# A feed-forward kernel: the first blocks of x fetched by DMA transpose instead of TensorE transposes, with chunk 1 and the last store rearranged

## The chip, the cores and the metric

The kernel runs on one core of a Trainium2 chip. The metric is the device time of one execution in microseconds (us). "Before" is the kernel as it was, "after" is the changed one.

A ratio is the mean time of one kernel's fast runs over the mean of the other's fast runs of the same rounds, so it is not quite the ratio of the medians that are also quoted. It comes with a 95% interval.

## The reference

```
def reference(x, w_gate, w_up, w_down):
    return (_gelu(x @ w_gate) * (x @ w_up)) @ w_down     # gelu: tanh form
# x: 32 x 32 x 1024, w_gate and w_up: 1024 x 3584, w_down: 3584 x 1024, all bf16
```

The 1024 tokens form two blocks of 512. The 1024 input columns form eight k blocks of 128. The kernel's matmuls contract over the partitions of their operands, so x is needed with its columns on partitions: transposed.

## The kernel before

The kernel multiplies 2 x 2 blocks by a Strassen-like scheme (sums S1 to S4 of the weights, T1 to T4 of x, seven products in place of eight). The first chunk of w_gate and w_up is computed plainly while the sums are formed. Names used below: `b21` holds the last four k blocks of x for the first 512 tokens; it is read first. `b11` holds the first four k blocks, `b12` and `b22` are the second 512 tokens. `a12a` is weights for products that are computed ahead. `w_tiles[0, ...]` is the first chunk of w_gate and w_up. PSUM banks come from three tags, A (4 banks), B (2) and C (2).

The head fetches the first two k blocks of b21 (`KQ = 2`) as they lie in memory and transposes them on TensorE. The other six come by DMA transpose:

```
    with tc.manual_schedule():
        for eng, p0, p1 in ((nc.sync, 0, HALF), (nc.scalar, HALF, NB_P)):
            eng.dma_start(out=x_nat[:, p0:p1, :],
                in_=xf[p0 * P : p1 * P, KD * P : (KD + KQ) * P].rearrange("(b p) d -> p b d", p=P))
        # [cut]
        for k, eng in enumerate((nc.sync, nc.scalar)):
            load_ahead(0, k, k + 1, eng)              # a12a, k block 0 and 1
        for which, eng in enumerate((nc.sync, nc.scalar)):
            load_w(eng, 0, which, KD, KD + KQ)        # w_gate, w_up for these k blocks
        load_xT(0, KD + KQ, DT)                       # DMA transpose, k blocks 2 and 3 of b21
        load_ahead(0, KQ, KD)
        load_w0(nc.sync, KD + KQ, DT)
        load_ahead(1, 0, KD)
        load_xT(0, 0, KD)                             # b11
        # [cut: w, b12, b22]
        warm_ps = acc("A")
        for _ in range(NWARM):                        # 6 matmuls on constants
            nc.tensor.matmul(warm_ps, lhsT=ones_w, rhs=ones_m, start=True, stop=True)
        # [cut: eight 128x128 TensorE transposes of x_nat, copied to b21; one half-size filler matmul]
```

Then the products start, one k block after the other:

```
        for k in range(KQ):
            for j in range(KB):
                product_ahead(ps[j], 0, j, k, k + 1)  # 4 matmuls per k block
        plain0(KD, KD + KQ)                           # 8 matmuls, token block 0
        for j, copy in enumerate((nc.scalar.copy, nc.vector.tensor_copy) * 2):
            product_ahead(ps[j], 0, j, KQ)            # k blocks 2 and 3: "third k block" below
            copy(ahead[0][:, j, :], ps[j])
```

Chunk 1, where the scheme begins, and the last bank of the output:

```
        # [cut: plain products of chunk 0]
        for j, tag in enumerate("BB"):
            ps = acc(tag)
            product_ahead(ps, 2, j)
            nc.scalar.copy(ahead[2][:, j, :], ps)
        tt(t3, b22, b12, SUB)
        begun = [first_product(FC + fl) for fl in range(FC)]   # P1, then added(...) on DVE frees the bank
        next(chunk1)                                           # S3
        tt(t4, b21, t2, SUB)
        # [cut: all chunks; S1 goes to bank C, S2 to the banks of P1]
        for copy, queue, c0 in ((nc.vector.tensor_copy, nc.sync, 0), (nc.scalar.copy, nc.scalar, NB // 2)):
            o = late.tile([P, NB // 2], bf16, name="o_end", tag="o_end", bufs=2)
            copy(o, banka[m][:, c0 : c0 + NB // 2])
            queue.dma_start(out=of[r0 : r0 + P, c0 : c0 + NB // 2], in_=o)
```

## Time and profile before

| | before |
|---|---|
| median of the first 3 runs | 275.81 us (275.01 to 275.81) |
| span in the profile | 273.6 us |
| PE busy | 269.1 us (98%) |
| first real product | 4.58 us |
| third k block starts | 8.03 us |
| last bank's copy starts | 270.02 us |

The profiled execution took 275.36 us, a little under the median.

The page's first part gives, for each engine, busy time, share of the span and instructions; a later line gives DMA packets by size.

```profile
span 273.6 us, 3349 instructions
...
PE 269.1 (98%) x1199; PEld 187.9 (69%) x1199; DVE 198.1 (72%) x195; ACT 111.4 (41%) x183; POOL 108.1 (40%) x55
...
DMA packets 53393, 33.77 MB, mean 123 GB/s; under 512 B 8704, under 2 KB 53376, under 8 KB 53376
```

The view of waits, of PE alone over the whole span, has one line: only the start of the program is waited for.

```profile
PE psA L224 <- PEq L582: 0.8, 1, 0.8
```

The matmuls wait for nothing else; weight loads (PEld) have waits of their own. What is left to win is the head, short stalls and the tail. The timeline shows the head; its columns are start, duration, engine, line, operation, result and operands, count, and in brackets the idle time before and what ended it. SPq and ACTq are the issues of DMAs on the two queues.

```profile
0.77 2.72 PE L224 MATMUL psA<-const-bfloat16-1.0 128*128 128x512 bf16 x6 [0.77 <-PEq L582]
...
2.21 1.56 SPq L205 DMA_TRANSPOSE b<-in_x_dram  x1
...
3.51 0.90 PE L232 MATMUL tp<-ident,x_nat 128*128 128x128 bf16 x8
...
4.58 0.59 PE L273 MATMUL psC<-b,a12a 128*128 128x512 bf16 x2
...
7.98 1.45 PEld L273 LDWEIGHTS <-a12a 128*128 128x128 bf16 x8 [0.28 <-DMA a12a<-in_w_gate_dram]
8.03 1.03 PE L273 MATMUL psC<-b,a12a 128*128 128x512 bf16 x4
```

The six warm-ups take 0.43 us apiece, the products 0.216 us apiece (two in 0.59 us: they start 0.216 us apart, and the record of one lasts 0.38 us). The page's row of granted clock prints full speed from the first slice on, so the slow clock of the start has to be read from such spacings; the trace's clock records (the array `clock` in the packed trace, which no view prints) give full clock from 4.13 us.

Chunk 1 in the timeline: DVE's t3 at 27.91 us stands ahead of the additions at 30.11 us, and the matmul group that needs the banks they free starts 2.27 us after its forerunner (28.57 to 30.84); later in this trace the same step takes 2.02 us where nothing is waited for (36.18 to 38.20). The waits of the weight loads name the cause (PEld, 16 to 50 us):

```profile
PEld psA L258 <- DVE c L335: 0.5, 1, 0.5
```

The timeline of DVE and PE:

```profile
27.91 2.29 DVE L355 TENSOR_TENSOR t<-b,b 128x2048 fp32r<-128x2048 bf16 x1
28.57 2.21 PE L258 MATMUL psC<-t,s 128*128 128x512 f32 x8
30.11 1.28 DVE L335 TENSOR_TENSOR c<-ahead,psA 128x512 f32<-128x512 f32 x2
30.84 2.11 PE L258 MATMUL psA<-t,s 128*128 128x512 f32 x8
```

The tail in the timeline: ACT's half copy waits for DVE's, so the last store is issued at 270.88 us.

```profile
270.02 0.42 DVE L568 CAST o_end<-psA 128x256 bf16<-128x256 f32 x1 [0.90 <-PE psA L421]
270.47 0.36 SPq L569 DMA_DIRECT2D out_dram<-o_end  x1
270.48 0.37 ACT L568 CAST o_end<-psA 128x256 bf16<-128x256 f32 x1 [3.04 <-DVE o_end L568]
270.88 0.34 ACTq L569 DMA_DIRECT2D out_dram<-o_end  x1
```

### The profile page before, as it was taken

The page shows a single profiled execution, that of the slowest core. Times are in us where ns is not written, and L with a number is a line of the kernel's source. Part 1 is how long each engine was busy: PE and PEld are TensorE (multiplying, and loading weights), DVE is VectorE, ACT ScalarE, POOL GpSimd, SP SyncE. Part 2 cuts the span into 40 slices and gives each one's busy share as a digit, 9 for nine tenths or more (in the row PEclk, how much of TensorE's full clock was granted, in tenths as well). Part 3 has the DMA queues.
Part 4 walks back from the last instruction along what each step waited for, and adds up shares of the span by engine and source line. Part 5 has one row for each costly group of instructions (what it writes and reads, how often), then busy time and mean ns, then how long its engine had stood idle before and what let it go on. Part 6 is the DMA issues. An engine that isn't in the chain of part 4 may idle for free.

```text
span 273.6 us, 3349 instructions
## 1 busy us (share of the span) xinstructions
PE 269.1 (98%) x1199; PEld 187.9 (69%) x1199; DVE 198.1 (72%) x195; ACT 111.4 (41%) x183; POOL 108.1 (40%) x55
## 2 busy tenths in 40 slices
PE   8999999999999999999999999999999999999994
PEld 3444677877878677676868676764447888888883
DVE  0269997987966676666657656459999999999511
ACT  2263565454643646555463636430300023962001
POOL 1000089999897695948577574000000000000000
PEclk9999999999999999999999999999999999999999
DMA  7994330414504505050514280004992445695202
GB/s 173 282 240 127 101 90 25 117 42 114 156 16 137 146 8 157 0 153 1 154 35 120 74 274 0 0 2 163 350 293 79 134 134 189 216 285 194 78 0 78
DMA packets 53393, 33.77 MB, mean 123 GB/s; under 512 B 8704, under 2 KB 53376, under 8 KB 53376
## 3 DMA queue, kind: packets, MB, share of 16 engines
q1 hardware_dynamic: 50384, 31.13, 39.4%
q10 hardware_dynamic: 2992, 2.43, 2.7%
q8 instruction: 9, 0.15, 0.2%
q14 instruction: 8, 0.07, 0.1%
HBM read 29.62 MB, written 2.10 MB: 116 GB/s over the span
## 4 chain that ended last, share of the span: by engine, by line
PE 87%; SPq 5%; DVE 4%; DMA 2%; issue 1%; ACT 0%; DVEq 0%
PE psA L258 34%; PE psA L421 18%; PE psC L258 17%; PE psC L421 7%; PE psB L421 7%; PE psB L258 5%; SPq L205 3%; DMA b<-in_x_dram 2%; DVE lo L254 1%; SPq L134 1%; DVE t L355 1%; DVE t L317 1%; SPq L194 1%; DVE s L163 0%; DVE s L162 0%
## 5 line engine op out<-in xcount | busy, mean ns | idle before, releaser
L258 PE MATMUL psA<-t,s 128*128 128x512 f32 x208 | 54.3, 403 | 0.1
L250 ACT ACTIVATE h<-c 128x512 bf16<-128x512 f32 x52 | 31.8, 630 | 38.9 <-DVE c L335 38.9
L258 PEld LDWEIGHTS psA<-t,s 128*128 128x128 f32 x208 | 39.0, 188 | 9.7 <-DVE c L335 0.5
L162 POOL TENSOR_TENSOR s<-wu 128x1024 fp32r<-128x1024 bf16 x12 | 26.8, 2232 | 23.4 <-DMA wu<-in_w_up_dram 14.0
L335 DVE TENSOR_TENSOR c<-sn,psA 128x512 f32<-128x512 f32 x26 | 17.8, 683 | 16.8 <-PE psA L258 16.5
L258 PEld LDWEIGHTS <-wg 128*128 128x128 bf16 x168 | 15.4, 98 | 20.1 <-issue 3.4
L163 POOL TENSOR_TENSOR s<-s,wg 128x1024 fp32r<-128x1024 f32 x12 | 27.8, 2314 | 0.9
L165 POOL TENSOR_TENSOR s<-wg,wu 128x1024 fp32r<-128x1024 bf16 x12 | 27.1, 2255 | 0.0
L340 ACT COPY sn<-psC 128x512 f32<-128x512 f32 x26 | 15.2, 588 | 27.1 <-PE psC L258 23.0
L340 ACT COPY sn<-psA 128x512 f32<-128x512 f32 x42 | 23.4, 585 | 6.2 <-PE psA L258 6.1
L258 PE MATMUL psC<-t,s 128*128 128x512 f32 x104 | 25.9, 391 | 0.0
L258 PE MATMUL psA<-t,a22r 128*128 128x512 f32 x104 | 25.9, 391 | 0.0
L258 PE MATMUL psC<-b22r,s 128*128 128x512 f32 x104 | 25.7, 389 | 0.0
L258 PE MATMUL psA<-b,wg 128*128 128x512 bf16 x104 | 24.6, 380 | 0.0
L258 PEld LDWEIGHTS psC<-t,s 128*128 128x128 f32 x104 | 19.5, 188 | 4.2
L258 PEld LDWEIGHTS psA<-t,a22r 128*128 128x128 f32 x104 | 19.5, 188 | 4.1
L258 PEld LDWEIGHTS psC<-b22r,s 128*128 128x128 f32 x104 | 19.5, 188 | 4.1
L400 DVE TENSOR_TENSOR lo<-c,h 128x512 bf16<-128x512 f32 x12 | 21.5, 1794 | 0.6
L335 DVE TENSOR_TENSOR c<-sn,psC 128x512 f32<-128x512 f32 x26 | 17.7, 687 | 5.1 <-PE psC L258 5.1
L353 DVE TENSOR_TENSOR hi<-h,psA 128x512 bf16<-128x512 bf16 x14 | 9.6, 688 | 14.2 <-PE psA L258 14.2
L164 POOL TENSOR_TENSOR s<-wg,s 128x1024 fp32r<-128x1024 bf16 x8 | 17.3, 2159 | 0.6
L464 ACT COPY snb<-psC 128x512 f32<-128x512 f32 x4 | 2.2, 590 | 36.5 <-PE psC L421 22.7
(101 smaller groups left out, 411.9 us busy)
## 6 DMA issues: line engine op xcount, KB each, us to landing
wu<-in_w_up_dram SPq DMA_DIRECT2D x13, 512.0 KB, 4.0
wdb<-in_w_down_dram SPq DMA_DIRECT2D x12, 512.0 KB, 4.8
wdb<-in_w_down_dram SPq DMA_DIRECT2D x12, 384.0 KB, 4.1
wg<-in_w_gate_dram SPq DMA_DIRECT2D x8, 512.0 KB, 5.1
v<-in_w_down_dram SPq DMA_DIRECT2D x4, 512.0 KB, 6.4
out_dram<-o_sb ACTq DMA_DIRECT2D x15, 128.0 KB, 1.7
wg<-in_w_gate_dram SPq DMA_DIRECT2D x6, 256.0 KB, 4.5
v<-in_w_down_dram SPq DMA_DIRECT2D x4, 384.0 KB, 7.8
```

What stands on the lines that cost most here:

```text
L162: yield eng.tensor_tensor(s1, a21, a22, ADD)
L163: yield eng.tensor_tensor(s2, s1, a11, SUB)
L164: yield eng.tensor_tensor(s4, a12, s2, SUB)
L165: yield eng.tensor_tensor(s3, a11, a21, SUB)
L205: nc.sync.dma_start_transpose(out=t[:, d0 % KD : (d1 - 1) % KD + 1, :], in_=xf[nb * NB : (nb + 1) * NB, d0 * P : d1 * P])
L250: nc.scalar.activation(h, src, ACT.Gelu_apprx_tanh)
L258: nc.tensor.matmul(ps, lhsT=lhs[:, k, :], rhs=rhs[:, k, :], start=(start and k == 0), stop=(k == KD - 1), skip_group_check=True,)
L335: tt(t, s, ps, ADD)
L340: nc.scalar.copy(t, ps)
L353: tt(g_of(ft)[:, :NB], h0, psa, MUL)
L400: tt(g_of(ft)[:, NB:], added(sn5[fl], psa[fl]), h1[fl], MUL)
L421: nc.tensor.matmul(banks[m], lhsT=lhs(k)[:, m * P : (m + 1) * P], rhs=rhs(k), start=(start and k == 0), stop=(k == HF - 1), skip_group_che ...
```

## The change

The intent: fetch the first two k blocks by DMA transpose too, one tile per DMA, with all transposes on the sync queue and the first weights on the scalar queue; this frees TensorE, DVE and ACT of the transposes and their copies. In chunk 1, P1 comes before the products ahead, and its additions before T3, S3 and T4. The last bank is copied and stored whole.

```
-    NWARM = 6
+    NWARM = 7
@@ head
-        for eng, p0, p1 in ((nc.sync, 0, HALF), (nc.scalar, HALF, NB_P)):
-            eng.dma_start(out=x_nat[:, p0:p1, :], ...)
-        for k, eng in enumerate((nc.sync, nc.scalar)):
-            load_ahead(0, k, k + 1, eng)
-        for which, eng in enumerate((nc.sync, nc.scalar)):
-            load_w(eng, 0, which, KD, KD + KQ)
+        for k in range(KQ):
+            load_xT(0, KD + k, KD + k + 1)
+            load_ahead(0, k, k + 1, nc.scalar)
+        load_w0(nc.scalar, KD, KD + KQ)
         load_xT(0, KD + KQ, DT)
-        # the eight TensorE transposes, their four copies, the filler matmul
@@ chunk 0 and 1   [cut: plain_out of token block 1 moved behind t4; its banks A and B, not A and C]
-        tt(t1, b12, b11, SUB)
         for fl in range(FC):
             ...
+            if fl == 0:
+                tt(t1, b12, b11, SUB)
+        p1 = [acc("A") for _ in range(FC)]
+        for fl in range(FC):
+            prod(p1[fl], quads(1, fl)[0], b11, True)
+        for j, tag in enumerate("CC"):
+            ps = acc(tag)
+            product_ahead(ps, 2, j)
+            nc.scalar.copy(ahead[2][:, j, :], ps)
+        begun = [first_product(FC + fl, p1[fl]) for fl in range(FC)]
         tt(t3, b22, b12, SUB)
-        begun = [first_product(FC + fl) for fl in range(FC)]
@@ tail
-            if m < MT - 1: ...            # and the split of the last bank in two halves
+            o = late.tile([P, NB], bf16, name="o_sb", tag="o_sb", bufs=MT)
+            (nc.vector.tensor_copy if m % 2 == 0 else nc.scalar.copy)(o, banka[m])
+            nc.scalar.dma_start(out=of[r0 : r0 + P, :NB], in_=o)
```

More of the change, by code (lines that the diff above doesn't have):

```diff
@@ L6 @@
 from concourse._compat import with_exitstack
-from concourse.masks import make_identity
 ACT = mybir.ActivationFunctionType
@@ L176 @@
     ones_m = nc.const_aps.tensor(1.0, [P, NB], bf16)
-    ident = xpool.tile([P, P], bf16, name="ident")
-    make_identity(nc, ident)
-    NB_P = NB // P
-    HALF = NB_P // 2
-    x_nat = spool.tile([P, NB_P, KQ * P], bf16, name="x_nat", tag="s1")
-    with tc.manual_schedule():
-        for eng, p0, p1 in ((nc.sync, 0, HALF), (nc.scalar, HALF, NB_P)):
-            eng.dma_start(
-                out=x_nat[:, p0:p1, :],
-                in_=xf[p0 * P : p1 * P, KD * P : (KD + KQ) * P].rearrange("(b p) d -> p b d", p=P),
-            )
+    gate = xpool.tile([P, 1], f32r, name="gate")
+    with tc.manual_schedule():
         alloc_w(0, 0)
@@ L224 @@
             nc.tensor.matmul(warm_ps, lhsT=ones_w, rhs=ones_m, start=True, stop=True)
-        tags = iter("CCBB")
-        for dt in range(KQ):
-            for half in range(2):
-                hw = HALF * P
-                tag = next(tags)
-                tp = ps1.tile([P, hw], bf16, name="tp", tag=tag, bufs=BANKS[tag])
-                for b in range(HALF):
-                    nc.tensor.transpose(
-                        tp[:, b * P : (b + 1) * P], x_nat[:, half * HALF + b, dt * P : (dt + 1) * P], ident
-                    )
-                (nc.vector.tensor_copy, nc.scalar.copy)[half](b21[:, dt, half * hw : (half + 1) * hw], tp)
-        nc.tensor.matmul(warm_ps[:, : NB // 2], lhsT=ones_w, rhs=ones_m[:, : NB // 2], start=True, stop=True)
         def plain(ps, which, fl, nb, d0, d1, first=0, last=DT - 1):
@@ L251, in gelu, with plain_out @@
             return h
-        def plain_out(ft, nb, gate, up):
-            tt(g_of(ft)[:, nb * NB : (nb + 1) * NB], gelu(gate, "h0", 4), up, MUL)
+        def plain_out(ft, nb, h, up):
+            tt(g_of(ft)[:, nb * NB : (nb + 1) * NB], h, up, MUL)
         def prod(ps, lhs, rhs, start):
@@ L311 @@
                 plain(tok0[fl][which], which, fl, 0, 0, KD, KD, KD - 1)
-            plain_out(fl, 0, *tok0[fl])
-        tok1 = [(acc("A"), acc("C")) for _ in range(FC)]
+            plain_out(fl, 0, gelu(tok0[fl][0], "h0", 4), tok0[fl][1])
+            if fl == 0:
+                tt(t1, b12, b11, SUB)
+        tok1 = [(acc("A"), acc("B")) for _ in range(FC)]
         for fl in range(FC):
@@ L324 @@
                 plain(tok1[fl][which], which, fl, 1, KD, DT)
-            plain_out(fl, 1, *tok1[fl])
+            tok1[fl] = gelu(tok1[fl][0], "h0", 4), tok1[fl][1]
         load_w_all(2, 1)
-        for j, tag in enumerate("BB"):
-            ps = acc(tag)
-            product_ahead(ps, 2, j)
-            nc.scalar.copy(ahead[2][:, j, :], ps)
         def added(s, ps):
@@ L341, in snap, with first_product @@
             return t
-        def first_product(ft):
-            psa = acc("A")
-            prod(psa, quads(*divmod(ft, FC))[0], b11, True)
+        def first_product(ft, psa=None):
+            if psa is None:
+                psa = acc("A")
+                prod(psa, quads(*divmod(ft, FC))[0], b11, True)
             if ft < FC + NAHEAD:
@@ L353, in last_product @@
             tt(g_of(ft)[:, :NB], h0, psa, MUL)
+        p1 = [acc("A") for _ in range(FC)]
[6 more added lines that the diff above has]
+        begun = [first_product(FC + fl, p1[fl]) for fl in range(FC)]
         tt(t3, b22, b12, SUB)
-        begun = [first_product(FC + fl) for fl in range(FC)]
         next(chunk1)
         tt(t4, b21, t2, SUB)
-        nc.gpsimd.tensor_copy(ident[:, :1], t4[:, 0, :1])
+        nc.gpsimd.tensor_copy(gate, t4[:, 0, :1])
+        for fl in range(FC):
+            plain_out(fl, 1, *tok1[fl])
         open_fts = []
@@ L559 @@
             r0 = NB + m * P
-            if m < MT - 1:
-                o = late.tile([P, NB], bf16, name="o_sb", tag="o_sb", bufs=MT)
-                (nc.vector.tensor_copy if m % 2 == 0 else nc.scalar.copy)(o, banka[m])
-                nc.scalar.dma_start(out=of[r0 : r0 + P, :NB], in_=o)
-                continue
-            for copy, queue, c0 in ((nc.vector.tensor_copy, nc.sync, 0), (nc.scalar.copy, nc.scalar, NB // 2)):
-                o = late.tile([P, NB // 2], bf16, name="o_end", tag="o_end", bufs=2)
-                copy(o, banka[m][:, c0 : c0 + NB // 2])
-                queue.dma_start(out=of[r0 : r0 + P, c0 : c0 + NB // 2], in_=o)
+            o = late.tile([P, NB], bf16, name="o_sb", tag="o_sb", bufs=MT)
+            (nc.vector.tensor_copy if m % 2 == 0 else nc.scalar.copy)(o, banka[m])
+            nc.scalar.dma_start(out=of[r0 : r0 + P, :NB], in_=o)
 _INS = ['x', 'w_gate', 'w_up', 'w_down']
```

## The prediction

> **What bounds the kernel now.** TensorE. The page gives PE 269.1 us busy of a 273.6 us span, and the waits view knows no PE wait on DMA, DVE or ACT. In the timeline matmuls start every 0.216 us (bf16) or 0.227 us (f32) from 4.58 us to 270.0 us. The change removes none of these real matmuls, so it can only move the head (first product at 4.58 us), small stalls between chunks, and the tail (270.0 to 273.6 us).
>
> **The head.** Before: six warm-up matmuls (0.77 to 3.49 us), x_nat lands 2.7 us after issue, eight transposes and a filler fill 3.51 to 4.52 us, product at 4.58. After that the head is paced by loads rather than by the transposes: the first w_gate block lands at about 6.05 (used at 6.10) and the next a12a block at 7.92, where the weight load waits 0.28 us. The DMA engines are saturated from 3 us to 21 us (share 1.0 or more in the windows view).
>
> After the change the first transpose issues at 0.74. The existing two-tile transpose held the queue 1.56 us and its first packets ran 2.0 us after issue (x_nat's: 1.1). I estimate issue 0.8 us per tile, data from 2.7 us, first tile landing at 4.4 (4.0 to 5.0), second near 5.2, the pair near 6.6. The scalar queue's a12a and w blocks no longer wait behind x, so w lands earlier, near 5. First product about 4.6; the next a12a block is issued near 4.0 (before 3.82) and lands at 8.0 to 8.5. In DMA time, x_nat cost 512 packets of 28 ns; two transposed tiles cost 1024 packets of 18 to 39 ns in this trace, over 16 engines 0.3 to 1.5 us more. [...] these packets (256 B at 18 ns against 512 B at 28) show them slower per byte. So removing the PE transposes gains nothing: PE then waits for DMA instead. Head: +0.1 us (-0.3 to +0.7).
>
> **Chunk 1.** DVE's t3 (2.29 us, 27.9 to 30.2) delays the additions; PE's weight load waits 0.50 us for c, matmul S1 to S2 takes 2.27 instead of 2.02 us, so 0.25 us is lost. With P1 before the a12b products, additions run near 26.5 to 27.8, ahead of t3; this wait should vanish. The new bank reuse (ahead copy of C, 0.59 us, before S1 into the same bank) has near 0.1 us slack. Gain 0.2.
>
> **Tail.** The last bank's split copies run one after the other (0.42, 0.37; last store issued at 270.88). One 0.59 us copy lets it issue at 270.6. Gain 0.1 to 0.2.
>
> **Sum.** +0.1 - 0.2 - 0.15: about -0.3 us. I predict 275.5 us (275.81 before; range 274.6 to 276.5). Faster by over 2%: 0.5%; within 2%: 98.5%; slower: 1%.
>
> **What would show it.** First real product between 4.3 and 5.0; PE waiting on DMA (b21 or a12a) in the first 9 us; P1 and S1 of chunk 1 back to back, no wait on c; Pool's sums starting 1 us earlier without effect; last store issued at 270.6 minus the shift; PE still near 98%.
>
> **What would make it wrong.** The first transposes take over 5.5 us to land: the head loses 1 us or more. The warm-up ends at about 3.8 and PE idles; [...] (full clock began at 4.1 us in this trace), so an idle gap could delay full clock [...]. Or the scalar queue's loads arrive so much earlier that PE starts by 4.2 and never waits: 0.5 us gained.

## The result, and the profile after

| | before | after |
|---|---|---|
| median | 275.81 us (275.01 to 276.0, 6 runs) | 276.4 us (276.0 to 277.24, 6 runs) |
| ratio, 95% interval | | 1.0031 [1.001, 1.0052] |
| span in the profile | 273.6 us | 275.4 us |
| first real product | 4.58 us | 4.71 us |
| third k block starts | 8.03 us | 10.37 us |
| S1 to S2 in chunk 1 | 2.27 us | 1.95 us |
| last bank's copy starts | 270.02 us | 272.05 us |
| from there to the end of the span | 3.6 us | 3.4 us |

The change made the kernel 0.6 us slower by the medians, clear of the interval, though far within 2%. The profiled execution of after was the slowest of its six (277.24 us), which matters below. The lines of the page:

```profile
span 275.4 us, 3319 instructions
...
PE 270.4 (98%) x1191; PEld 187.9 (68%) x1191; DVE 192.5 (70%) x192; ACT 111.2 (40%) x181; POOL 106.5 (39%) x53
...
DMA packets 53793, 33.77 MB, mean 123 GB/s; under 512 B 9744, under 2 KB 53776, under 8 KB 53776
```

There are some 1000 more packets under 512 B: two transposed tiles of 512 rows. The waits of PE have a second line now:

```profile
PE psC L252 <- DMA b<-in_x_dram: 0.8, 1, 0.8
PE psA L215 <- PEq L561: 0.8, 1, 0.8
```

The timeline of the head:

```profile
0.74 3.89 SPq L195 DMA_TRANSPOSE b<-in_x_dram  x3
...
0.78 3.14 PE L215 MATMUL psA<-const-bfloat16-1.0 128*128 128x512 bf16 x7 [0.78 <-PEq L561]
...
4.71 1.01 PE L252 MATMUL psC<-b,a12a 128*128 128x512 bf16 x2 [0.79 <-DMA b<-in_x_dram]
...
5.51 1.06 PE L252 MATMUL psA<-b,a12a 128*128 128x512 bf16 x2
...
6.54 1.01 PE L252 MATMUL psC<-b,a12a 128*128 128x512 bf16 x2
...
10.37 1.03 PE L252 MATMUL psC<-b,a12a 128*128 128x512 bf16 x4
```

Pairs of products now take 1.01 to 1.06 us where they took 0.59: they run at half clock. The clock records give full clock from 9.09 us in place of 4.13. Chunk 1 in the timeline, where the wait has gone:

```profile
31.07 2.12 PE L237 MATMUL psC<-t,s 128*128 128x512 f32 x8
33.02 1.98 PE L237 MATMUL psA<-t,s 128*128 128x512 f32 x8
```

The tail in the timeline: one copy, and the store follows 0.61 us after the copy's start (before: 0.86).

```profile
272.05 0.58 ACT L547 CAST o_sb<-psA 128x512 bf16<-128x512 f32 x1 [2.59 <-PE psA L407]
272.66 0.34 ACTq L548 DMA_DIRECT2D out_dram<-o_sb  x1
```

So in this execution the head lost 2.34 us (8.03 to 10.37), chunk 1 won 0.3 and the tail 0.2. Two theories for the head offer themselves, and they are not exclusive. **A**: TensorE sits idle for 0.79 us between the warm-ups and the first product, and that postpones the full clock. **B**: the second transposed tile lands late, so that TensorE would have to wait even at full clock. A rival, **C**, blames the rearranged chunk 1. Where B's cure was tried, a further rival **D** says that all loads of the head are late and the wait only moves.

### The profile page after: what moved, and what is told of

It reads as the page before. It is cut to its first block, busy times and chain, and to the rows that moved or that the text cites. A ratio compares the mean times of both kernels' runs of the same rounds, so it can differ in the third digit from the quotient of the medians.

```text
span 275.4 us, 3319 instructions
## 1 busy us (share of the span) xinstructions
PE 270.4 (98%) x1191; PEld 187.9 (68%) x1191; DVE 192.5 (70%) x192; ACT 111.2 (40%) x181; POOL 106.5 (39%) x53
## 4 chain that ended last, share of the span: by engine, by line
PE 97%; DMA 1%; ACT 0%; issue 0%
PE psA L237 34%; PE psA L407 18%; PE psC L237 17%; PE psC L407 7%; PE psB L407 7%; PE psB L237 5%; PE psA L219 3%; PE psB L219 3%; PE psC L252 2%; PE psA L252 2%; DMA b<-in_x_dram 1%; ACT o_sb L547 0%
## 5 line engine op out<-in xcount | busy, mean ns | idle before, releaser
L386 DVE TENSOR_TENSOR lo<-c,h 128x512 bf16<-128x512 f32 x12 | 18.1, 1509 | 0.6
```

The costliest lines, as they stand in the source:

```text
L386: tt(g_of(ft)[:, NB:], added(sn5[fl], psa[fl]), h1[fl], MUL)
```

## The experiments

Eleven runs were made, all correct, each with 5 or 6 fast executions beside 11 of before (mean of before: 275.78, 275.71 and 275.64 us in the three calls). Names with a_ are edits of after, with b_ of before.

| kernel | median us | mean us | ratio to before [95%] | full clock from, in the profile | third k block |
|---|---|---|---|---|---|
| before (first profile) | 275.81 | 275.64 | | 4.13 us | 8.03 |
| after | 276.4 | 276.50 | 1.0031 [1.001, 1.0052] | 9.09 | 10.37 |
| a_again | 276.22 | 276.46 | 1.0029 [1.001, 1.0047] | 4.34 | 9.13 |
| a_warm9 | 276.13 | 276.22 | 1.0019 [1.0, 1.0037] | 5.82 | 9.13 |
| a_pair | 275.88 | 276.18 | 1.0018 [0.9995, 1.0042] | 3.97 | 9.01 |
| a_fill9 | 275.77 | 275.78 | 1.0004 [0.999, 1.0018] | 6.11 | 8.86 |
| a_pair_w | 275.76 | 275.72 | 1.0002 [0.9987, 1.0016] | 5.82 | 8.86 |
| b_head | 277.67 | 277.67 | 1.007 [1.005, 1.0089] | 9.04 | 10.51 |
| b_head_warm9 | 276.8 | 276.88 | 1.0044 [1.0032, 1.0056] | 3.57 | 9.35 |
| b_warm4 | 276.46 | 276.54 | 1.0028 [1.0009, 1.0048] | 8.54 | 10.06 |
| b_rest | 275.29 | 275.27 | 0.9983 [0.9966, 0.9999] | 6.13 | 8.86 |
| b_rest_again | 275.23 | 275.35 | 0.9989 [0.9977, 1.0002] | 4.94 | 8.29 |
| b_rest_third | 275.11 | 275.13 | 0.9978 [0.9964, 0.9992] | 3.49 | 7.82 |

### b_head and b_rest: which part of the change costs

b_head is before with the hunk of the diff marked "head" and `NWARM = 7` alone. b_rest is before with all the other hunks (chunk 0 and 1, tail), `NWARM = 6` and the old head:

```
b_head = before + (NWARM, head)
b_rest = before + (chunk 0 and 1, tail)
after  = before + (NWARM, head) + (chunk 0 and 1, tail)
```

> The kernel before with only the head of the change (DMA transposes, seven warm-ups). Theory A: the loss is here, 276.5 to 277.2 (0.5 us slower than after, since it lacks the gains of chunk 1 and the tail). Rival B: the same time. Rival C: as before, 275.6 to 276.0.

> The kernel before with only the rest of the change (chunk 1 order and the undivided last store). Theories A and B: faster than before by 0.4 to 0.6 us (0.32 from chunk 1, 0.23 from the tail, as the two traces show), 275.2 to 275.4. Rival C: slower than before by 0.3 to 0.8.

Measured: the head alone costs 0.7%, 1.9 us by the means. The rest alone wins 0.17%, 0.5 us. Theory C falls. But the two do not add up: 1.9 - 0.5 gives 1.4, and after is only 0.75 to 0.86 us slower by the means. Two reasons offer themselves, and neither is shown. The reordering of chunk 1 may be worth more behind the new head; b_head_warm9 below looks like that, but b_head's own profile does not. Its timeline at chunk 1, PE alone:

```profile
31.04 2.19 PE L237 MATMUL psC<-t,s 128*128 128x512 f32 x8
33.07 1.98 PE L237 MATMUL psA<-t,s 128*128 128x512 f32 x8
```

From S1 to S2 that is 2.03 us, with nothing lost. Or the full clock came late more often in b_head: five of its six executions took 277.47 us or more, while in after five of twelve were slow (see a_again). Only one profile of b_head was kept, so this stays open; so does why b_head came out 0.5 us above the range expected for it. (The 0.23 us that the text above gives the tail is too much: from the last copy to the end of the span the two traces show 3.55 and 3.40 us.)

### b_warm4: the gap alone

```
-    NWARM = 6
+    NWARM = 4
```

> The kernel before with four warm-ups in place of six: nothing changes in the loads, but TensorE idles about 1.0 us (2.5 to 3.5 us) before the transposes. Theory A: the full clock starts later than 4.1 us, at 7 to 9 us, in most executions, and the time rises by 0.5 to 1.8 us over before. Rival B: no change (within 0.3), since the first transpose still starts when x lands.

Nothing but two warm-ups was taken from before, and the loads are the same. The timeline of b_warm4, PE alone:

```profile
0.77 1.87 PE L224 MATMUL psA<-const-bfloat16-1.0 128*128 128x512 bf16 x4 [0.77 <-PEq L582]
3.57 1.14 PE L232 MATMUL tp<-ident,x_nat 128*128 128x128 bf16 x8 [0.93 <-DMA x_nat<-in_x_dram]
...
7.28 1.06 PE L273 MATMUL psA<-b,a12a 128*128 128x512 bf16 x2
```

TensorE idles 0.93 us, the first eight products run at half clock (a pair in 1.06 us), the full clock starts at 8.54 us, and the kernel is 0.76 us slower by the means (the profiled execution, 277.04 us, is one of the slower of the six). So an idle stretch of this length in the head can cost time by the clock alone. Theory A's mechanism is there.

### a_warm9: the gap bridged

```
-    NWARM = 7
+    NWARM = 9
```

> The kernel after with nine warm-up matmuls in place of seven, so that TensorE has no idle stretch between the warm-up and the first product. Theory A (the idle 0.79 us delays the full clock): in the profile the products start at the same time (4.6 to 4.8 us) but run at 0.216 us spacing from there or soon after, and the time falls by 0.8 to 1.8 us against after, to 274.6 to 275.6. Rival B (the head is held by the later loads, the clock is only a passenger): the time stays within 0.3 us of after, 276.1 to 276.7, and TensorE waits for a12a, w or b instead. Rival C (the loss is in the reordered chunk 1): also no change.

The gap is gone and the full clock starts at 5.82 us. But the mean falls by 0.28 us only, from 276.50 to 276.22 (0.31 to 0.42 against each one's own runs of before; the intervals overlap), where theory A expected 0.8 to 1.8. The timeline of a_warm9, PE alone, shows why:

```profile
5.59 0.71 PE L252 MATMUL psA<-b,a12a 128*128 128x512 bf16 x2
6.54 0.59 PE L252 MATMUL psC<-b,a12a 128*128 128x512 bf16 x2 [0.24 <-DMA b<-in_x_dram]
...
9.13 1.03 PE L252 MATMUL psC<-b,a12a 128*128 128x512 bf16 x4
```

The products of the second tile start at 6.54 us, the same time as in after. The clock is faster, and TensorE waits for the tile instead. The prediction for a_warm9 was wrong in size, and theory A alone is not enough. It was also held against an execution of after with a late clock, and not all of them have one, as the next run shows.

### a_again: after once more, with a lucky clock

No edit.

> The kernel after, unchanged, to see how its executions spread and a second profile of it. Theory A (the idle gap delays the full clock): the full clock starts at 7.8 us or later in this profile too, and the times lie at 276 to 277.3. Theory B (the second transposed tile lands late, 1.9 us after the first, so that TensorE would wait for it even at full clock): the second product group starts at 6.5 to 6.9 us whatever the clock does; the two are not exclusive.

Theory A's number for this run failed: TensorE was idle for the same stretch (3.91 to 4.72 us), but the full clock came in the middle of it, at 4.34 us. That makes it the cleanest view of theory B, and the right one to hold against the profile of before (full clock at 4.13). The waits of PE, and the timeline of the head:

```profile
PE psC L252 <- DMA b<-in_x_dram: 1.6, 2, 0.8
```

```profile
4.72 0.59 PE L252 MATMUL psC<-b,a12a 128*128 128x512 bf16 x2 [0.80 <-DMA b<-in_x_dram]
...
5.15 0.59 PE L252 MATMUL psA<-b,a12a 128*128 128x512 bf16 x2
...
6.54 0.59 PE L252 MATMUL psC<-b,a12a 128*128 128x512 bf16 x2 [0.80 <-DMA b<-in_x_dram]
...
9.13 1.03 PE L252 MATMUL psC<-b,a12a 128*128 128x512 bf16 x4
```

The first four products are done in 0.86 us, and then the second tile is still 0.8 us away. From 6.54 us the twelve products at 0.216 us give 9.13 us exactly, so no other load holds the head. At full clock the head thus costs 9.13 - 8.03 = 1.10 us. The rest of the two traces: S2 of chunk 1 starts at 31.77 us against 30.84 (now 0.93 behind), the last bank's copy at 270.80 against 270.02 (0.78 behind), and the span ends at 274.2 against 273.6 (0.6 behind). This is 1.10 lost, 0.32 won around chunk 1 (about half of it before S2, the rest in the group after it) and 0.15 won in the tail (with the spans unrounded, 273.574 and 274.199 us). The two profiled executions took 275.36 and 275.98 us. The medians also differ by 0.6 us, but each of them mixes earlier and later clocks, so that the two agree may be chance; by the means, after is 0.86 us slower in the first call and 0.75 in the second.

The twelve executions of after fall into two groups: seven from 275.77 to 276.22 us and five from 276.68 to 277.44. One profile fell into each: 275.98 us with full clock at 4.34, and 277.24 us with full clock at 9.09. Their third k blocks lie 10.37 - 9.13 = 1.24 us apart, their times 1.26 us. So between these two a late clock costs that much on top. That the other ten split for the same reason is likely, but no profile of them was kept. It would also fit a_warm9: its mean, 276.22, lies near that of the fast group, 276.05 (the slow group: 277.07).

### b_head_warm9: the head with the gap bridged, on before

b_head with `NWARM = 9`.

> The kernel before with the head of the change alone and nine warm-ups. Theory A: 0.8 to 1.5 us faster than b_head (277.67 median), 276.2 to 276.9, with the full clock at 4.2 to 7.6 us. Theory B alone: no faster than b_head by more than 0.4 us.

It is 0.79 us faster than b_head by the means (0.72 when each is held against its own runs of before): just short of what theory A expected, and more than theory B alone allowed. The full clock starts at 3.57 us, earlier than expected, in the middle of the warm-ups; so in this profile it does not come from a bridged gap, and TensorE even sits idle from 4.25 to 4.87 us. The timeline of it, PE alone, at chunk 1:

```profile
29.89 2.20 PE L237 MATMUL psC<-t,s 128*128 128x512 f32 x8
32.42 2.12 PE L237 MATMUL psA<-t,s 128*128 128x512 f32 x8 [0.34 <-DVE c L314]
```

Without the reordering of chunk 1, S1 to S2 takes 2.53 us here, 0.50 more than the 2.03 of b_head, where nothing was waited for; before lost 0.25 (2.27 against 2.02). So the two parts of the change are not independent, but how they act on each other depends on the clock: in b_head TensorE reached S1 1.15 us later (31.04 against 29.89), DVE began the additions 0.28 us sooner (31.41 against 31.69), and there was nothing left for the reordering to mend.

### a_pair: one transpose for both tiles

```
-    NWARM = 7
+    NWARM = 10
+        load_xT(0, KD, KD + KQ)
         for k in range(KQ):
-            load_xT(0, KD + k, KD + k + 1)
             load_ahead(0, k, k + 1, nc.scalar)
```

> The kernel after with the first two tiles fetched by one DMA transpose in place of two, and ten warm-ups to bridge until it lands. Theory B: the pair needs one issue (about 1.3 us) instead of two, lands at 5.0 to 5.5 us, the eight first products follow without a gap, and the products of the third and fourth k block start at 8.5 to 8.9 us (9.13 in a_warm9, 7.98 before); the time falls by 0.3 to 0.7 us against a_warm9, to 275.5 to 275.9. Theory A alone: as a_warm9, 276.1 to 276.3.

The issues say why the second tile was late. In after, the three transposes of the head hold the sync queue 1.25, 1.25 and 1.29 us, for one, one and two tiles. So an issue was hardly cheaper here with half the tiles (1.25 against 1.29). They land 3.9, 4.5 and 4.0 us after their issue, at 4.7, 6.5 and 7.3 us. The lines of the first two, from the DMA view (tile, queue, operation, count, us from issue to landing) and, for the second, its issue in the timeline:

```profile
b<-in_x_dram SPq DMA_TRANSPOSE x1, 3.9
...
2.04 1.25 SPq L195 DMA_TRANSPOSE b<-in_x_dram  x1
...
b<-in_x_dram SPq DMA_TRANSPOSE x1, 4.5
```

Of the 1.83 us between the two landings, 1.30 are the distance of the issues and 0.53 the longer way from issue to landing; the packets of the second tile (3.72 to 5.27 us) ran beside those of w_gate and w_up, those of the first (2.16 to 3.18) before them. In a_pair one issue of 1.34 us brings both tiles in 4.3 us, at 5.0 us. The timeline, PE alone:

```profile
5.08 0.59 PE L252 MATMUL psC<-b,a12a 128*128 128x512 bf16 x2 [0.42 <-DMA b<-in_x_dram]
...
6.80 1.03 PE L219 MATMUL psA<-b,wg 128*128 128x512 bf16 x4
8.13 1.04 PE L219 MATMUL psB<-b,wu 128*128 128x512 bf16 x4 [0.30 <-DMA wu<-in_w_up_dram]
9.01 1.03 PE L252 MATMUL psC<-b,a12a 128*128 128x512 bf16 x4
```

The wait for the second tile is gone, as theory B expected. But w_up, from the scalar queue, now lands at 8.1 us (after: 6.2), 6.0 us after its issue (before: 4.5), and the third k block starts at 9.01 us, only 0.12 us sooner. Here rival D was right: the wait moved. In the packet records of the first 8 us, the 512 B packets of the scalar queue take 51 ns apiece by the mean, where in before they took 28; the median is 27 ns in both, so it is some packets that are held up for long. The median time, 275.88 us, is in theory B's range, but one of the six executions took 277.95 us, and the third k block is later than it expected.

### a_pair_w: the order mended

a_pair with the first w blocks on the sync queue, between the pair and the second pair of tiles:

```
-        load_w0(nc.scalar, KD, KD + KQ)
+        load_w0(nc.sync, KD, KD + KQ)
```

> a_pair with the first two w blocks issued on the same queue as the transposes, between the pair and the second pair, in place of the scalar queue, so that they do not share the DMA engines with the second pair. In a_pair the wait had moved to w_up (8.13 us). Theory B with order: w lands at 5.6 to 6.5, no wait, the third k block starts at 8.5 to 8.7 (9.01 in a_pair), the time is 275.5 to 275.8. Rival D (total DMA time): the third k block starts at 8.9 or later because a12a lands late, 275.9 to 276.2.

PE waits for no load any more. The third k block starts at 8.86 us, between the two ranges; but the full clock came at 5.82 us in this profile, and the first two products took 0.85 us in place of 0.43. The pair had landed at 4.55 us already; the ten warm-ups at half clock kept TensorE until 4.99 us. By the means it is 0.46 us faster than a_pair, but by the medians 0.12 (most of the difference is a_pair's one slow execution; ratio 1.0002 against 1.0018, the intervals overlap), so the times decide nothing. Theory B with order fits better than rival D, since no load was waited for.

### a_fill9: only TensorE reordered

```
-    NWARM = 7
+    NWARM = 9
         for k in range(KQ):
             for j in range(KB):
                 product_ahead(ps[j], 0, j, k, k + 1)
-        plain0(KD, KD + KQ)
+            plain0(KD + k, KD + k + 1)
```

> The kernel after with nine warm-ups, and TensorE alone reordered: between the products of the first and of the second tile it now does the four token products that need only the first tile; all loads stay as they are. Theory B (the late second tile is what holds the head at full clock): the four products take 0.86 us of the wait, the third k block starts at 8.3 to 8.7 us in place of 9.13, and the time falls by 0.4 to 0.8 us against a_warm9 (276.22 mean), to 275.4 to 275.8. Rival D (the DMA engines as a whole are late, and the second tile is only the first of many late loads): the wait moves to the next load (w or a12a), the third k block still starts near 9.0, and the time stays at 276.0 to 276.3.

All loads are as in after and a_warm9. TensorE alone does other work while the second tile is on its way. The timeline, PE alone:

```profile
4.75 1.01 PE L252 MATMUL psC<-b,a12a 128*128 128x512 bf16 x2
...
7.13 0.59 PE L252 MATMUL psC<-b,a12a 128*128 128x512 bf16 x2
...
8.86 1.03 PE L252 MATMUL psC<-b,a12a 128*128 128x512 bf16 x4
```

The wait for x is gone from the waits of PE, and no other took its place there (one weight load waits 0.2 us for w_up without holding the matmuls up), although the full clock came only at 6.11 us: the first products took 6.27 - 4.75 = 1.52 us in place of 0.86. That is why the third k block starts at 8.86 and not at the expected 8.3 to 8.7. The median of 275.77 us lies in theory B's range and outside rival D's, and the five executions agree within 0.12 us. Against a_warm9 the mean falls by 0.44 us (against each one's own runs of before by 0.30; the intervals of the two ratios overlap, every execution of a_fill9 lies below every one of a_warm9, 275.85 against 275.99, but before differed by 0.14 us between the two calls). The times alone would not settle it. In the two profiles the third k block moves by 0.27 us, 9.13 to 8.86, about the 0.24 us that a_warm9 waited for the tile. So the late second tile did hold the head.

### b_rest_again and b_rest_third: the better version

No edit against b_rest.

> The kernel before with the head left alone and the rest of the change, once more, as the candidate for the best version: 275.1 to 275.5, 0.3 to 0.6 us faster than before, which the interval of the ratio should now show below 1.

> The candidate for the best version a third time, for its interval: 275.1 to 275.5, ratio to before 0.998 to 0.9995.

With the old head and the rest of the change, the kernel is faster than before by 0.36 to 0.51 us by the means in three calls; the interval lies below 1 in two of the three (not in b_rest_again, for which it was expected; in b_rest_third the ratio is just below its expected range). It is the best version here, and all kernels are the same within 2%. Its three profiles have the full clock from 6.13, 4.94 and 3.49 us and the third k block at 8.86, 8.29 and 7.82 us: the old head has no gap, but it is not free of the clock either.

## Why the prediction was right or wrong

- **The sum was wrong in sign.** It forecast 0.3 us less; the medians show 0.6 us more. The range (274.6 to 276.5) held 276.4, just.
- **What bounds the kernel: right.** PE stays at 98%; only head, stall and tail moved.
- **The failed step is the head's term, "+0.1 us (-0.3 to +0.7)".** At full clock it measures 1.10 us (a_again). Its first half was right: first product "about 4.6", measured 4.71; first tile at 4.4 (4.0 to 5.0), measured 4.7; the next a12a "at 8.0 to 8.5", measured 8.2. What failed is "issue 0.8 us per tile" and "second near 5.2". I had divided the 1.56 us of a two-tile transpose by two; a one-tile transpose holds the queue 1.25 us. The second tile then took 4.5 us from issue to landing and came at 6.5 us. With its own 5.2 the twelve products between the second tile and the third k block would have been done at 7.8 us, before its a12a of 8.0 to 8.5, and +0.1 follows; with 6.5 they are done at 9.13, behind an a12a of 8.2 to 8.5, and that is the 1.10. So the order of need was implied rightly, and the term that was mis-sized is the landing of the second tile.
- **"PE then waits for DMA instead": right** as a mechanism, by b21, 1.6 us in a_again. Of a12a, the other load named, no matmul waited.
- **The clock: named as a risk, left out of the sum.** That "an idle gap could delay full clock" was an estimate, not yet shown, when it was written. It happened in the profile of after (0.79 us idle, full clock from 9.09 us) and cost 1.24 us against a_again; the times suggest that it happened in 5 of 12 executions. b_warm4 shows the same by the gap alone (0.93 us idle, full clock from 8.54). The term belonged in the sum with a probability, since the same text predicted the gap: warm-up ending at 3.8 and the product at 4.6.
- **"w lands earlier, near 5": half right.** w_gate landed at 5.1 us, w_up at 6.2. Neither was waited for in after.
- **Chunk 1, "gain 0.2": right,** measured 0.32. The bank reuse on C was not quite free: the weight load of S1 waited 0.3 us for the copy, and from the last product before S1 to S1's third matmul 0.76 us went by in a_again, 0.69 in before. (S1 so starts later, which is why S1 to S2 takes 1.95 us in after and 2.03 in b_head.)
- **Tail, "gain 0.1 to 0.2": right,** measured 0.15 in a_again.
- **Pool's sums: wrong in time.** Its gate opened only 0.3 us earlier (34.89 before, 34.61 in a_again) and not 1 us, since the head had shifted everything. As predicted, no wait of PE shows an effect of it.

In the trace of before a 256 B transpose packet takes 18 or 38 ns by the mean of a tile (median 18) against 28 ns for a plain 512 B one (median 27), so per byte they are slower, but that did not decide: it was the issue and the landing of a small transpose. A transpose of one 128-column tile of 512 rows (128 KB) held the queue 1.25 us in after, one of two tiles 1.24 to 1.74 us in these runs, a plain DMA of 128 KB 0.39 us (the first of after) to 0.71 us (w_up in a_pair). In after the first tile landed 3.9 us after its issue; x_nat, a plain 128 KB in before, after 2.7 and 2.9 us on the two queues.

In these profiles the length of the idle stretch alone does not tell when the full clock comes. With 0.79 us of it between warm-up and first product in after, 0.82 in b_head and 0.93 before the transposes in b_warm4, the full clock came at 9.09, 9.04 and 8.54 us. With 0.80 us in a_again it came in the middle of the stretch, at 4.34. Once there, it outlasted the last matmul: it held for 269.65 us in before and 266.24 in after, and in b_head_warm9 (full clock from 3.57 us) it stayed through two idle stretches of the head, 0.62 and 0.88 us. What decides when it comes is not shown.

What stays open: why head and rest do not add up (b_head is a few tenths slower than its parts explain), and why a transposed tile lands some 1.5 us after its last packet (3.2 to 4.7 us for the first tile of after).

## What to carry to other kernels

A small DMA transpose cost its issue and landing here, and hardly its bytes (1.25 us of issue for one tile, 1.24 to 1.74 for two; in after 3.9 and 4.5 us to landing for one, 4.0 for two): price it by an issue of the same size, and lay each landing against the order in which TensorE will need it, because moving work off an engine that was never waiting gains only if the replacement arrives in time. When the start of a kernel leaves TensorE idle between warm-up and first product, put the clock into the sum and not among the risks (a late full clock cost 1.24 us here, after against a_again), bridge the gap, and look at the spread of the times. If a tile must land late, give TensorE the work that needs only what is there (a_fill9) before you rearrange loads.
